# A ring of five expert slots on the chip, hand-ordered engines, half-partition stores and a column-tiled tail in an attention-plus-experts kernel

## The chip, the cores and the metric

The kernel runs on one core of one Trainium2 chip. The metric is the device time of one execution in microseconds (us). The kernel before takes 252.5 us (median; its runs spread from 252.4 to 253.2).

Engine names in the profile: PE is TensorE's matmuls, PEld its weight loads (beside the matmuls: 7.9 us of them in a stage of 16.7 us that PE fills), DVE is VectorE, ACT is ScalarE, POOL is GpSimd. L171 is line 171 of the kernel that the profile belongs to. "MoE" is the expert part of one sequence.

## The reference, cut to what matters

Eight sequences of 576 tokens go through a linear attention with 8 heads of 64 and then, whole, through one of eight experts. The mean of the attention's output picks the expert.

```python
# attention: q, k, v are [8 sequences, 8 heads, 576, 64]
q_s = softmax(q, axis=-1)                 # over the 64 of a head
k_s = softmax(k, axis=2)                  # over the 576 tokens
kv  = einsum('bhsd,bhse->bhde', k_s, v)
x   = einsum('bhsd,bhde->bhse', q_s, kv)  # then [8, 576, 512]
# experts: w1 [8, 512, 1024], w2 [8, 1024, 512]
e_idx  = argmax(x.mean(axis=1) @ w_gate, axis=1)
out[b] = gate_w[b] * (relu(x[b] @ w1[e]) @ w2[e])
```

With the inputs used here the eight sequences draw the experts 2 3 3 1 3 3 4 6, so three of the eight weight loads repeat an expert already drawn.

## The kernel before

Attention runs two sequences ahead of the experts. A sequence is prepared in two halves: exponentials on ScalarE, row sum, reciprocal and multiply on VectorE. TensorE transposes the result, VectorE copies it out as `qt`, and a matmul with `kv` gives `x`. Only TensorE's order is given by hand, one attention step after each MoE step. The compiler orders all other engines.

```python
# attention(b), one half
qs = tensor_reduce(eq, add); qsi = reciprocal(qs)
nc.vector.tensor_tensor(out=eq, in0=eq, in1=qsi..., op=ALU.mult)   # both halves first
...
tps = [bank(t_tag, 2) for g in range(2)]          # two transpose banks
for j in range(J):
    for g in range(2):                            # row groups alternate
        nc.tensor.transpose(out=tps[g]..., in_=eq[r, j], identity=ident[r, r])
...
# routing, then every sequence loads its expert
e_val = nc.values_load(eidx[0:1, 0:1], engines=[ET.Pool], ...)
nc.gpsimd.dma_start(out=w1_sb[...], in_=w1_src[i, h])              # 4 such, then 2 for w2
...
# moe(b): 8 steps of W1, 4 steps of W2 with 128 rows, a tail with 64 rows
nc.scalar.mul(osb[0:rows], po[0:rows], gate[0:rows])
nc.sync.dma_start(out=out[b, st * 128:...], in_=osb[0:rows])       # same queue as the inputs
...
with tc.manual_schedule(engines={ET.PE}):
    for b in range(B):
        ...
        for step, _ in enumerate(moe(b)):
            next(att, None)
```

The softmax here doesn't subtract the row's maximum and nothing guards it: scores larger than these inputs give would overflow.

## Time and profile before

| what | before | from |
|---|---|---|
| median time | 252.5 us | the runs |
| profiled span, mean granted clock | 251.7 us, 0.959 | the cores view |
| first MoE starts | 45.6 us | the timeline |
| lengths of the seven stages after it | 27.3, 43.3, 25.6, 25.6, 24.0, 22.5, 16.7 us | the same |
| last MoE starts | 230.7 us | the same |

A stage runs from the first W1 matmul of one MoE to that of the next. A mixed stage has an attention woven in; the last two stages have none. The second stage holds a hole, which the waits view explains (columns: who waits, for what, us in total, times, longest). One result store had not landed for 19.6 us, so ScalarE could not write the next result, and TensorE stood still behind it for 16.0 us:

```profile
PE hm L243 <- ACT hsb L253: 16.0, 1, 16.0
ACT osb L269 <- DMA out_dram<-osb: 19.6, 1, 19.6
```

The prediction below shows the other lines of this profile.

### The profile page before, as it was taken

What the parts mean: (1) busy time and instruction counts of PE and PEld (TensorE: products, weight loads), DVE (VectorE), ACT (ScalarE), POOL (GpSimd) and SP (SyncE); (2) the same over time, 40 slices, a digit from 0 to 9 for tenths busy, and PEclk for the clock granted to TensorE, in tenths of its full rate; (3) what the DMA queues carried; (4) which work ended last, traced back from release to release, by engine and by line L of the source; (5) the groups of instructions that cost most, each with busy time, mean ns of one, the idle gap of its engine ahead of it and who ended that gap; (6) DMA issues with size and microseconds to landing.
All of it is one profiled execution on the core that took longest, in us unless ns stands there. A gap on an engine that the chain in (4) does not pass through costs nothing.

```text
span 251.7 us, 4145 instructions
## 1 busy us (share of the span) xinstructions
PE 184.3 (73%) x1552; PEld 92.9 (37%) x1552; DVE 131.4 (52%) x365; ACT 91.1 (36%) x130; POOL 52.5 (21%) x73
## 2 busy tenths in 40 slices
PE   0234342887991028799779977997999899999993
PEld 0221221444441004444444444444544454544541
DVE  0699999399411018932993299419723760210300
ACT  3535521335220042535352535353233133344332
POOL 1331451612331000142113211231041006000000
PEclk9999999999997556999999999999999999999999
DMA  6999999999999978669998992299339907993023
GB/s 223 391 392 393 388 296 285 293 283 281 294 282 279 292 204 282 173 174 200 279 316 284 195 240 37 49 177 244 54 74 205 236 11 153 225 188 131 19 83 104
DMA packets 31956, 54.81 MB, mean 218 GB/s; under 512 B 2752, under 2 KB 10944, under 8 KB 31936
## 3 DMA queue, kind: packets, MB, share of 16 engines
q1 hardware_dynamic: 18304, 37.75, 42.5%
q0 software_dynamic: 13056, 16.78, 40.6%
q8 instruction: 12, 0.20, 0.3%
q10 hardware_dynamic: 576, 0.02, 0.1%
q14 instruction: 8, 0.07, 0.1%
HBM read 61.88 MB, written 9.44 MB: 283 GB/s over the span
## 4 chain that ended last, share of the span: by engine, by line
PE 47%; DVE 37%; DMA 11%; ACT 2%; issue 1%; ACTq 1%; DVEq 0%
PE po L264 27%; PE hm L243 12%; DMA out_dram<-osb 8%; DVE qt L154 8%; DVE qs L131 8%; DVE eq L134 7%; DVE xt L184 5%; DVE hsb L255 3%; DMA wg_sb<-in_moe_w_gate_dram 2%; DVE kv L173 2%; PE tk L147 2%; PE x L182 1%; DVE xt L188 1%; PE ht L248 1%; DVE qsi L133 1%
## 5 line engine op out<-in xcount | busy, mean ns | idle before, releaser
L243 PE MATMUL hm<-xt,w_sb 128*128 128x512 f16 x256 | 69.0, 397 | 16.0 <-ACT hsb L253 16.0
L264 PE MATMUL po<-w_sb,hsb 128*128 128x512 f16 (+1 forms) x320 | 73.4, 380 | 0.0
L269 ACT ACTIVATE osb<-po,gate 128x512 f32<-128x512 f32 (+1 forms) x40 | 27.4, 686 | 68.0 <-PE po L264 44.5
L264 PEld LDWEIGHTS <-hsb 128*128 128x128 f16 (+1 forms) x320 | 29.9, 100 | 35.0 <-issue 3.4
L126 POOL CAST va<-v_in 128x1152 f16<-128x1152 f32 x16 | 20.1, 1264 | 94.5 <-PE tk L164 40.6
L154 DVE COPY qt<-tk 128x576 f16<-128x576 f16 x24 | 17.1, 753 | 38.9 <-PE tk L147 38.9
L243 PEld LDWEIGHTS <-w_sb 128*128 128x128 f16 x256 | 20.9, 100 | 39.9 <-issue 21.9
L255 DVE TENSOR_SCALAR hsb<-hm 128x512 f16<-128x512 f32 x32 | 21.9, 686 | 25.7 <-PE hm L243 25.7
L253 ACT ACTIVATE hsb<-hm 128x512 f16<-128x512 f32 x32 | 18.9, 592 | 42.2 <-PE hm L243 42.2
L131 DVE TENSOR_REDUCE qs<-eq 128x18 f32<-128x1152 f16 x16 | 21.5, 1342 | 24.3 <-ACT eq L115 24.3
L211 POOL DMA_DIRECT2D w_sb<-in_moe_w_dram x32 | 19.3, 622 | 64.6 <-DVE gt L225 45.6
L248 PEld LDWEIGHTS <-w_sb 128*128 128x128 f16 x256 | 16.8, 101 | 16.4 <-issue 2.2
L120 ACT ACTIVATE ek<-k_in 128x1152 f16<-128x1152 f32 x16 | 18.5, 1159 | 11.9 <-PE tk L164 8.9
L115 ACT ACTIVATE eq<-q_in 128x1152 f16<-128x1152 f32 x16 | 18.6, 1161 | 11.5 <-DMA q_in<-in_q_dram 5.6
L134 DVE TENSOR_TENSOR eq<-eq,qsi 128x1152 f16<-128x1152 f16 x16 | 21.9, 1368 | 0.1
L164 PE MATMUL tk<-va,ek 64*128 64x129 f16 x288 | 16.0, 246 | 5.0 <-DVE qt L154 2.9
L248 PE MATMUL ht<-xt,w_sb 128*128 128x64 f16 x256 | 18.5, 196 | 0.0
L182 PE MATMUL x<-qt,kv 128*128 128x512 f16 x24 | 9.6, 401 | 10.8 <-DVE pooled L184 5.8
L184 DVE CUSTOM_DVE_ANT_0 xt<-x,ones_f 128x512 f16<-128x512 f32 x24 | 16.4, 685 | 1.6 <-PE tk L183 1.6
L164 PEld LDWEIGHTS <-ek 64*128 64x128 f16 x288 | 11.3, 108 | 7.7 <-issue 6.5
L147 PEld LDWEIGHTS <-eq 64*128 64x128 f16 x288 | 6.5, 103 | 13.4 <-ACT wg_sb L89 9.4
L182 PE MATMUL po<-qt,kv 128*128 128x512 f16 x8 | 4.4, 612 | 9.5 <-DVE kv L173 9.5
(49 smaller groups left out, 107.9 us busy)
## 6 DMA issues: line engine op xcount, KB each, us to landing
q_in<-in_q_dram SPq DMA_DIRECT2D x16, 576.0 KB, 10.6
k_in<-in_k_dram SPq DMA_DIRECT2D x16, 576.0 KB, 11.6
v_in<-in_v_dram SPq DMA_DIRECT2D x16, 576.0 KB, 11.5
w_sb<-in_moe_w_dram POOLq DMA_DIRECT2D x32, 256.0 KB, 7.9
w_sb<-in_moe_w_dram POOLq DMA_DIRECT2D x16, 512.0 KB, 14.6
out_dram<-osb SPq DMA_DIRECT2D x32, 256.0 KB, 4.1
out_dram<-osb SPq DMA_DIRECT2D x8, 128.0 KB, 6.0
wg_sb<-in_moe_w_gate_dram ACTq DMA_DIRECT2D x4, 4.0 KB, 5.4
```

The lines of the kernel that those rows point to most:

```text
L126: nc.gpsimd.tensor_copy(out=va[:, :, 1:].rearrange("p j (n d) -> p n j d", n=2), in_=tiles["v", i].rearrange("p n (j d) -> p n j d", j=J),)
L131: nc.vector.tensor_reduce(out=qs, in_=eq, op=ALU.add, axis=AX.X)
L134: nc.vector.tensor_tensor(out=eq, in0=eq, in1=qsi.unsqueeze(3).to_broadcast([128, J, 2, Dh]), op=ALU.mult,)
L154: nc.vector.tensor_copy(out=qt.rearrange("q (p j) -> q p j", j=J), in_=tps[g].bitcast(FP16)[:, 0:S].rearrange("q (j p) -> q p j", j=J),)
L164: nc.tensor.matmul(kps[g][:, 0:129], lhsT=ek[r, j], rhs=va[r, j], start=(j == 0), stop=(j == J - 1),)
L184: nc.vector.tensor_tensor_reduce(out=xt[:, c, 0:SM], in0=px, in1=ones_f32.to_broadcast([128, SM]), scale=1.0, scalar=0.0, op0=ALU.mult, op ...
L211: nc.gpsimd.dma_start(out=w1_sb[64 * h:64 * h + 64, 2 * i:2 * i + 2, :], in_=w1_src[i, h])
L243: nc.tensor.matmul(phm, lhsT=w1_sb[:, c, fsl], rhs=xt[:, c, 0:SM], start=(c == 0), stop=(c == ND - 1),)
L248: nc.tensor.matmul(pht[:, fc * ST:(fc + 1) * ST], lhsT=w1_sb[:, c, fsl], rhs=xt[:, c, SM:S], start=(fc == 0 and c == 0), stop=(fc == NF - ...
L255: nc.vector.tensor_single_scalar(out=hsb[:, fc, 0:SM], in_=phm, scalar=0.0, op=ALU.max)
L264: nc.tensor.matmul(po[0:rows], lhsT=hsb[:, fc, st * 128:st * 128 + rows], rhs=w2_sb[:, fc, :], start=(fc == 0), stop=(fc == NF - 1),)
L269: nc.scalar.mul(osb[0:rows], po[0:rows], gate[0:rows])
```

## The change

The intent has four parts.

1. Keep the last five experts on the chip in a ring of slots. If the drawn expert is in a slot, skip its load and copy the slot on VectorE into the sequence's own slot.
2. Order all engines by hand, with input loads three half-sequences ahead instead of a sequence and more. Move the ReLUs to ScalarE and most of the multiplies to GpSimd.
3. Store results from 64 partitions at a time, in a token order that makes the `qt` copy dense.
4. Compute the W2 tail of 64 rows as two column halves side by side.

```diff
-    w_pool = ctx.enter_context(tc.tile_pool(name="w", bufs=3))
+    w1_all = consts.tile([128, NS, ND, F], FP16, name="w1_all")    # NS = 5
+    w2_all = consts.tile([128, NS, NF, D], FP16, name="w2_all")
+    BUFS = {"mm": 3, "ht": 1, "kv": 2, "t": 1, "x": 1}             # one transpose bank
...
+        eng = nc.vector if n < 4 else nc.gpsimd
+        eng.tensor_tensor(out=eq, in0=eq, in1=qsi..., op=ALU.mult)
...
-            tps = [bank(t_tag, 2) for g in range(2)]
+            for g in range(2):                                     # one group, then the other
+                tp = bank("mm" if roomy and g == 1 else "t").bitcast(FP16)
...
+            kw = dict(cond=(f_val == 1))                           # load only a fresh expert
+    def fetch(b, w_all):                                           # slot copy on VectorE
+        nc.vector.tensor_copy(out=w_all[:, b % NS], in_=w_all[:, ds(s_val, 1)]...)
...
+            for jj in range(2):
+                nc.sync.dma_start(out=out_p[b, :, 2 * st + jj], in_=osb[64 * jj:64 * jj + 64])
...
+        for fc in range(NF):
+            for dh in range(2):                                    # column-tiled tail
+                nc.tensor.matmul(po[64 * dh:64 * dh + 64, 0:HD], lhsT=hsb[:, fc, SM:S], ...)
...
-    with tc.manual_schedule(engines={ET.PE}):
+    with tc.manual_schedule(engines={ET.PE, ET.DVE, ET.Activation, ET.Pool, ET.SP}):
+        half_now = min(2 * b + (1 if s >= 1 else 0) + (1 if s >= 6 else 0), 2 * B - 1)
+        while prepared[0] <= half_now:                             # ahead of the step's own work
+            prepare_half(prepared[0])
+        if b and s == 6: fetch(b - 1, w1_all)
+        if b and s == 8: fetch(b - 1, w2_all)
+                owed = min(owed + 1.25, NA * (b + 3) - pos[0])     # attention steps per MoE step
```

## The prediction

> **What bounds the kernel now.** I read the page first: busy shares, the 40 slices, the DMA queues, the chain that ended last.
>
> ```profile
> PE 184.3 (73%) x1552; PEld 92.9 (37%) x1552; DVE 131.4 (52%) x365; ACT 91.1 (36%) x130; POOL 52.5 (21%) x73
> PE   0234342887991028799779977997999899999993
> DVE  0699999399411018932993299419723760210300
> DMA  6999999999999978669998992299339907993023
> q1 hardware_dynamic: 18304, 37.75, 42.5%
> q0 software_dynamic: 13056, 16.78, 40.6%
> PE 47%; DVE 37%; DMA 11%; ACT 2%; issue 1%; ACTq 1%; DVEq 0%
> ```
>
> No engine is full; the stages differ. Slices are 6.3 us. To slice 7 (45.7 us) PE works at 0.2 to 0.4 while DVE and DMA are full: a prologue of two attentions. Slices 12 to 14 hold a hole. Slices 15 to 33 mix one expert (MoE) with one attention, DVE alternating with PE. The last two MoEs are pure PE. Then I measured the stages with windows cut at MoE starts.
>
> ```profile
> 20.00:45.70 25.70, 9.31 (x105) 5.55 (x106) 24.31 (x66) 8.77 (x12) 8.68 (x11) 1.00 1.08 335
> 70.50:92.00 21.50, 5.87 (x63) 3.04 (x62) 2.02 (x3) 1.25 (x2) 1.90 (x2) 0.69 1.10 282
> 116.30:141.90 25.60, 22.16 (x195) 11.14 (x196) 16.08 (x45) 11.16 (x16) 6.24 (x8) 1.00 1.04 269
> 214.00:230.70 16.70, 16.70 (x106) 7.91 (x106) 2.77 (x4) 6.42 (x10) 0.00 (x0) 1.00 0.86 190
> ```
>
> Columns: stretch, length, busy PE, PEld, DVE, ACT, POOL, clock, DMA share, GB/s. A pure MoE takes 16.7 us, a mixed stage 25.6 (later 24.0 and 22.5). The hole at 70.5 is one store: the waits view has ScalarE's evacuation 19.6 us behind it, the DMA engines being full with loads ordered long ahead. Last, the timeline of one mixed stage gives the hand-offs.
>
> ```profile
> 117.82 1.16 ACT L115 ACTIVATE eq<-q_in 128x1152 f16<-128x1152 f32 x1
> 119.72 1.34 DVE L131 TENSOR_REDUCE qs<-eq 128x18 f32<-128x1152 f16 x1
> 122.98 0.68 DVE L184 CUSTOM_DVE_ANT_0 xt<-x,ones_f 128x512 f16<-128x512 f32 x1
> 123.72 0.38 PE L182 MATMUL x<-qt,kv 128*128 128x512 f16 x1 [0.73 <-DVE pooled L184]
> ```
>
> Exp 1.16 us and row sum 1.34 us stand in one chain; a second x matmul waits until DVE has emptied the only x bank.
>
> [...]GpSimd's first cast took 1.95 us while DVE's multiply ran from 7.90 to 9.26 us, later ones 1.17.[...]
>
> **The change part by part.**
> *Weights.* Running the reference's routing gives experts 2 3 3 1 3 3 4 6, so 5 of 8 loads remain. The software queue's 40.6% of 251.7 us x 5/8 leaves 64 us of DMA work; with the hardware queue's 107 that is 171 of 252 us instead of 209. Loads run three half-sequences ahead, not a whole sequence and more, so the store hole should vanish: -21 us. Without it this saving lies beside other work.
> *PE work.* [...]Attention stays near 3.6 us a sequence.
> *DVE work.* Leaves: 32 ReLUs (21.9 us) and 12 of 16 multiplies (16.4). Comes: 14 slot copies, run even when nothing is resident[...], and some eight small routing operations a sequence (about 1.2 us each time, 8 x 1.2 = 10). About 11 us less[...].
> *Prologue.* One and a half attentions before the first MoE. DVE's order: half 0 (sum and multiply) to 9.3 us, kv and half 1's preparation to 15.3, qt and xt to 18.5, kv to 20.5, half 2's preparation to 23.4, qt and xt to 26.5, routing to 29, then half 3 with its own preparation to 37. First MoE at about 38 (45.7 before).
> *The hand order in a mixed stage.* I had the compiled order of both kernels listed. PE: W1, kv, W1, transposes, W1, transposes, and so on. DVE: kv evacuation, **row sum of the next half, then the qt copies**. The exp for that sum stands on ScalarE behind the ReLU of the second W1 step, and there is now one transpose bank, so the second transposes wait for the first qt copy. From the end of that W1: ReLU 0.1 + 0.5, exp 1.1, sum 1.4, reciprocal 0.3, [...]hand-off 0.05 = 3.9 us; PE has 0.23 + 0.98 of work meanwhile: **2.7 us of wait**. Half a stage later the same chain has a slot copy in it[...]. Two x matmuls stand back to back on one bank: **0.9**[...]. The gate's matmul waits for routing: 2.95 us from its logits (1.26 in the old trace, plus six operations more and two for the split gate) against one W2 step of 1.75: about **1.4** with hand-offs. Sum 10.2. PE's work: 8 x 0.98 + 4 x 1.73 [...]+ 3.7 = 19.4. A mixed stage comes to 29.6, four more than before.
> *Sum.* 38 prologue; first stage (sixteen attention steps, three preparations, two slot copies) 33.5; second 30; three of 29.6 = 88.8; the last mixed one without its second preparation 25.8; two pure 31.4 to 32; end 3.2: 251. The hole's 21 us and the prologue's 8 would be given back by waits in the stages.
>
> **The rivals.** (A) As worked out, **251 us**: hand order makes row sums stand ahead of what PE needs. For: each duration is in the trace, and the order is in the program. Against: somebody tuned this order, and would have seen such waits; my chain takes every hand-off in full. (B) Half of these waits are hidden, because ScalarE and DVE run ahead or operations overlap: stages of 25 us, **224 us**. (C) PE becomes the bound: stages of 20.5 us, 195, plus some 10 us of late weight landings (in the old trace the second weight matrix landed 12.6 to 22.4 us after issue, and DVE now stands behind it): **205 us**. For: PE work falls and DVE is lighter. Against: one transpose bank and one x bank.[...]
>
> **Range and chances.** Weights 0.55, 0.25, 0.20 for A, B, C give a mean of 0.55 x 251 + 0.25 x 224 + 0.20 x 205 = 235; the middle of the distribution lies higher, as A is the heaviest, so I say 240. The range of 210 to 258 runs from C to A[...]. Faster by over 2% means below 247.5: all of B and C and 0.4 of A, 0.67. Slower (over 257.6): 0.08. Within 2%: 0.25.
>
> **What would show it.** Right: no hole of 20 us; software queue near 10.5 MB; first MoE near 38 us; PE waits of 2 us and more at the transposes, released by the qt copy, twice a stage; the qt copy behind the row sum in the chain of waits; mixed stages near 29 us[...]. Wrong: mixed stages of 20 to 22 us with PE above 90% (C), slot copies above 2 us or waits of DVE for weights (the prediction too low), or a first MoE later than 45 us.

Where the text is cut, it gave figures that no trace of the kernel before shows: what a slot copy, a dense `qt` copy, GpSimd's multiply and the column-tiled tail take, and a fourth rival and a remark that rested on them. So (A) did not have each duration from the trace. The sums still hold the cut terms: waits of 10.2 us (6.6 at the transposes, of which 2.7 at the first with the `qt` copy's term in it; 2.2 at the `x` matmuls; 1.4 at the gate), 19.4 us of PE's work with the tail in it, 29.6 us for a mixed stage, 251 us in all, and some 11 us less work on VectorE. The range's upper end, 258, holds the cut remark. That PE's work falls, in (C), was not shown either.

## The result and the profile after

The changed kernel takes **290.9 us** (median of four runs; the three fast ones from 289.9 to 291.5, a slow one of 298.4) against 252.5. The ratio is 1.150, with a 95% interval of 1.145 to 1.155. All ratios here are the mean time of one kernel's fast runs over that of the other's in the same rounds, so they are not quite the ratio of the medians quoted. The change was predicted faster and is 15% slower.

First the page of the changed kernel: busy time of the engines, three rows of 40 slices (here of 7.2 us), and the software DMA queue.

```profile
PE 197.5 (68%) x1608; PEld 102.6 (36%) x1608; DVE 132.5 (46%) x416; ACT 105.0 (36%) x161; POOL 68.0 (24%) x89
PE   0242376667577296673796649959289688899992
PEclk9999997999599787995997966986759959999999
DMA  7999899499917726997156261410007950798324
...
q0 software_dynamic: 8736, 10.49, 22.7%
```

The load saving came as designed: the software queue moved 10.49 MB instead of 16.78. The DMA row falls to 0 and 1 in the later slices, so transfers are not what bounds the kernel there. PE's row has no hole of several slices any more, but few of its slices are full before the last two MoEs, and two fall to 0.2. The row PEclk has changed: before, the mean granted clock was 0.959, with slices of 0.5 in and just after the hole alone; here it is 0.887, with 0.5 to 0.7 in many stages. The clock has no record before its first change at 42.4 us, and the views count full clock there. The 128x512 matmuls of that time take 0.58 to 0.63 us, as later at half clock (0.38 at full clock), so the mean is too high by this, in both kernels alike.

Next the windows cut at MoE starts (columns: stretch, length, busy PE, PEld, DVE, ACT, POOL, granted clock, DMA share, GB/s): two mixed stages and a pure one.

```profile
148.60:185.10 36.50, 26.82 (x203) 13.24 (x203) 17.07 (x51) 12.87 (x20) 6.76 (x10) 0.81 0.43 130
185.10:222.80 37.70, 28.03 (x204) 13.72 (x203) 17.07 (x51) 12.87 (x20) 9.47 (x10) 0.77 0.18 37
251.80:267.70 15.90, 15.90 (x115) 7.96 (x114) 2.45 (x2) 8.49 (x14) 0.17 (x1) 1.00 0.95 184
```

The six mixed stages, which took 22.5 to 27.3 us before (the hole apart), now take 38.8, 36.6, 33.2, 36.5, 37.6 and 29.1 (the second window above ends 0.1 us late); the pure stage shrank from 16.7 to 15.9. PE counts 26.8 and 28.0 us busy in these two, where a stage before had 22.2, though it has no more to compute: at the clocks of 0.81 and 0.77 its work takes longer. Both things can be seen in the timeline of the first of these stages (columns: start, length, engine, line, what; in brackets the wait before it and who ended it).

```profile
151.71 1.04 PE L293 MATMUL mm<-xt,w_all 128*128 128x512 f16 x4
153.01 1.35 DVE L132 TENSOR_REDUCE qs<-eq 128x18 f32<-128x1152 f16 x1 [1.64 <-ACT eq L126]
155.10 0.64 PE L171 MATMUL t<-ident,eq 64*128 64x64 f16 x9 [2.23 <-DVE qt L175]
155.66 1.89 PE L293 MATMUL mm<-xt,w_all 128*128 128x512 f16 x4
...
166.11 2.94 DVE L280 COPY w_all<-w_all 128x4096 f16 x1 [0.42 <-DVE qsi L134]
169.47 0.63 PE L171 MATMUL t<-ident,eq 64*128 64x64 f16 x9 [5.66 <-DVE qt L175]
173.81 3.60 PE L311 MATMUL mm<-w_all,hsb 128*128 128x512 f16 x8
```

PE waits 2.23 us for a `qt` copy that stands behind a row sum on VectorE, and 5.66 us for one that stands behind a row sum and a slot copy. After each wait the same W1 group takes 1.89 us instead of 1.04, and a W2 step 3.60 instead of the 1.90 that it took before. Windows of 3.41 us, laid so that they meet the clock's own changes, show how the two go together:

```profile
151.63:155.04 3.41, 1.23 (x13) 0.68 (x10) 1.93 (x3) 2.89 (x4) 0.14 (x1) 1.00 0.32 66
155.04:158.46 3.42, 3.15 (x19) 1.58 (x19) 0.69 (x3) 0.60 (x1) 3.08 (x2) 0.50 0.97 347
...
165.28:168.69 3.41, 0.00 (x0) 0.00 (x0) 2.88 (x3) 0.19 (x1) 2.12 (x1) 1.00 0.90 274
168.69:172.11 3.42, 2.64 (x18) 1.42 (x18) 2.41 (x4) 0.15 (x1) 0.00 (x0) 0.50 0.60 222
172.11:175.52 3.41, 2.68 (x10) 0.94 (x8) 1.98 (x8) 0.94 (x2) 0.00 (x0) 0.50 0.02 7
175.52:178.94 3.42, 3.42 (x17) 1.16 (x16) 1.01 (x8) 0.69 (x1) 0.00 (x0) 0.50 0.00 0
178.94:182.35 3.41, 3.15 (x16) 1.35 (x15) 1.20 (x10) 1.08 (x3) 0.22 (x5) 1.00 0.41 94
```

The clock is 1.00 or 0.50 for a whole window and changes only between two; the records of half clock in this trace are 3.413, 6.827 or 10.240 us long, one, two or three windows. PE was idle for 2.18 us of the first window (3.41 less 1.23), and the next one runs at half clock; that one has 0.27 us idle and is followed by full clock. The window that is idle throughout is followed by three at half clock: two of them still have 0.7 to 0.8 us of waits, and only after the third, with none, does the clock return.

I cut the whole changed kernel this way. Every change of its clock before the last MoE's end, 20 in all, lies within 0.05 of a whole number of windows of 3.413 us from the first. 19 windows, 64.9 us, are at half clock. PE was busy for 51.4 us of these, so its work took at most half of that, 26 us, longer for the clock.

Over the whole kernel the waits view names one wait above all, and the groups view shows the slot copies (busy us, mean ns of one, idle before):

```profile
PE t L171 <- DVE qt L175: 45.8, 13, 5.7
```

```profile
L280 DVE COPY w_all<-w_all 128x4096 f16 x14 | 25.0, 1788 | 18.7 <-DMA w_all<-in_moe_w_dram 14.8
```

The copies' mean of 1788 ns mixes two sizes: 1.23 us alone (the shortest is 1226 ns) and 2.94 us when one starts just after GpSimd's multiply (one that started 0.98 us after it took 2.22), as here in the timeline of an earlier stage:

```profile
96.08 2.12 POOL L136 TENSOR_TENSOR eq<-eq,qsi 128x1152 f16<-128x1152 f16 x1 [4.64 <-ACT hsb L304]
96.34 2.94 DVE L280 COPY w_all<-w_all 128x4096 f16 x1 [0.43 <-DVE qsi L134]
```

The copy ends 1.08 us after the multiply, which is roughly its time alone.

### The profile page after: what moved, and what is told of

The parts are those of the page before. It is cut to its first block, busy times and chain, and to the rows that moved or that the text cites. A ratio compares the mean times of both kernels' runs of the same rounds, so it can differ in the third digit from the quotient of the medians.

```text
span 288.6 us, 4585 instructions
## 1 busy us (share of the span) xinstructions
PE 197.5 (68%) x1608; PEld 102.6 (36%) x1608; DVE 132.5 (46%) x416; ACT 105.0 (36%) x161; POOL 68.0 (24%) x89
## 3 DMA queue, kind: packets, MB, share of 16 engines
q0 software_dynamic: 8736, 10.49, 22.7%
## 4 chain that ended last, share of the span: by engine, by line
PE 42%; DVE 12%; ACT 4%; issue 2%; DVEq 0%; ACTq 0%
PE mm L311 17%; PE mm L293 15%; DVE w_all L280 3%; DVE qs L132 3%; ACT eq L126 3%; PE mm L324 2%; DVE xt L184 2%; PE x L182 2%; PE kv L152 2%; PE t L171 2%; PE ht L298 2%; DVE qt L175 1%; DVE qsi L134 1%; ACT hsb L302 1%; PE x L196 0%
## 5 line engine op out<-in xcount | busy, mean ns | idle before, releaser
L293 PE MATMUL mm<-xt,w_all 128*128 128x512 f16 x256 | 75.0, 424 | 0.0
L302 ACT ACTIVATE hsb<-mm 128x512 f16<-128x512 f32 x64 | 38.1, 595 | 85.2 <-PE mm L293 85.2
L311 PE MATMUL mm<-w_all,hsb 128*128 128x512 f16 x256 | 66.9, 416 | 0.0
L171 PE MATMUL t<-ident,eq 64*128 64x64 f16 x270 | 15.2, 207 | 45.8 <-DVE qt L175 45.8
L316 ACT ACTIVATE osb<-mm,gate 128x512 f32<-128x512 f32 x32 | 22.0, 686 | 54.8 <-PE mm L311 33.8
L136 POOL TENSOR_TENSOR eq<-eq,qsi 128x1152 f16<-128x1152 f16 x12 | 25.4, 2115 | 68.7 <-DVE qsi L134 64.1
L311 PEld LDWEIGHTS <-hsb 128*128 128x128 f16 x256 | 25.1, 105 | 36.9 <-issue 14.4
L280 DVE COPY w_all<-w_all 128x4096 f16 x14 | 25.0, 1788 | 18.7 <-DMA w_all<-in_moe_w_dram 14.8
L293 PEld LDWEIGHTS <-w_all 128*128 128x128 f16 x256 | 21.8, 105 | 27.8 <-issue 12.9
L298 PEld LDWEIGHTS <-w_all 128*128 128x128 f16 x256 | 17.8, 105 | 18.3 <-issue 5.7
L159 DVE RECIPROCAL icv<-kv 128x1 f32<-128x1 f32 x32 | 5.2, 163 | 38.8 <-PE kv L152 38.8
L298 PE MATMUL ht<-xt,w_all 128*128 128x64 f16 x256 | 19.3, 201 | 0.0
```

The lines of the kernel that those rows point to most:

```text
L136: eng.tensor_tensor(out=eq, in0=eq, in1=qsi.unsqueeze(3).to_broadcast([128, J, 2, Dh]), op=ALU.mult,)
L171: nc.tensor.transpose(out=tp[:, 64 * j:64 * j + 64], in_=eq[r, j], identity=ident[r, r],)
L280: nc.vector.tensor_copy(out=w_all[:, b % NS], in_=w_all[:, ds(s_val, 1)].rearrange("p o c f -> p (o c) f"))
L293: nc.tensor.matmul(phm, lhsT=w1_sb[:, c, fsl], rhs=xt[:, c, 0:SM], start=(c == 0), stop=(c == ND - 1),)
L298: nc.tensor.matmul(pht[:, fc * ST:(fc + 1) * ST], lhsT=w1_sb[:, c, fsl], rhs=xt[:, c, SM:S], start=(fc == 0 and c == 0), stop=(fc == NF - ...
L302: nc.scalar.activation(out=hsb[:, fc, 0:SM], in_=phm, func=AF.Relu)
```

## The experiments

**Theory 1**: the hand order of the vector work makes PE wait at the second transposes (row sum and slot copy ahead of the `qt` copy), and these waits cost twice, because the clock halves after them. **Rival 2**: the waits belong to TensorE's own order and its single transpose bank, whatever the vector order. **Rival 3**: the ring itself is the loss. Twelve kernels ran, all with correct results; the ratio is always to the kernel before.

### Row sums after the qt copies

```diff
     def prepare_half(n): ...            # exponentials stay where they were
+    def sums_half(n): ...               # row sum, reciprocal, multiply
...
         next(att[b])
+        sum_now = min(2 * b + (1 if s >= 2 else 0) + (1 if s >= 7 else 0), 2 * B - 1)
+        while summed[0] <= sum_now:
+            sums_half(summed[0])
```

> Only VectorE's order is changed: the row sum, reciprocal and multiply of the next half stand behind the two qt copies instead of ahead of them; exps, slot copies and everything else stay. Theory of the hand order (the sum ahead of the qt copy makes TensorE wait at the second transposes, 2.2 us in the first half of a stage and 5.7 in the second): the 45.8 us of waits at the transposes fall below 10; about 1 us comes back per stage at the x matmuls in the first half, and in the second half the second slot copy now runs beside GpSimd's multiply, so some 4 to 5 us turn up at the x matmul there. Total about 268 us. Rival (the slot copies alone make the waits): first half as before, total 285 to 290.

Measured: **264.8 us**, ratio 1.048 (1.043 to 1.054), clock 0.951. From the waits view:

```profile
PE x L185 <- DVE pooled L187: 34.3, 14, 5.9
PE t L174 <- DVE qt L178: 4.4, 6, 1.7
```

The waits for `qt` fell from 45.8 to 4.4 us and the kernel gained 26 us by an edit of order alone. A new wait took 34.3 us: the second `x` matmul now stands behind the slot copy, 4.82 us in each steady stage. The steady mixed stages went from 33 to 38 us to 30.7.

### Slot copies later, row sums where they were

```diff
+        if b and s == 6:
+            fetch(b - 1, w1_all)        # ahead of the next half's row sum
         half_now = ...
-        if b and s == 6: fetch(b - 1, w1_all)
-        if b and s == 8: fetch(b - 1, w2_all)
         next(att[b])
+        if b and s == 9: fetch(b - 1, w2_all)
```

> Only the slot copies move: W1's goes ahead of the row sum, into the time in which VectorE waits for the exp, W2's behind the x evacuations. Theory of the slot copies: none runs beside GpSimd's multiply, so all take 1.23 us (now 2.95 in four to six of them); the second wait at the transposes falls from 5.7 to the 2.2 of the first, and with it most of the time at half clock behind it: mixed stages from 36 to about 30 us, total about 250 us. Rival (the row sum alone makes the wait, copies are hidden anyway): the second wait stays above 4 us, total above 275.

Measured: 272.4 and 271.6 us in two fast runs, 277.3 and 277.4 in two slow ones. All copies took 1.23 us, as they no longer met the multiply, and the wait of 5.66 us became 2.04 to 2.24. Yet the total missed the expectation by some 22 us. In two stages a wait of the same 2.24 us ended at 147.5 and at 192.5 us, and what came after differs (the first two lines are the 1.5 us after each wait; the other two are windows of the 3.413 us grid):

```profile
147.50:149.00 1.50, 1.45 (x12) 0.81 (x12) 0.46 (x1) 0.00 (x0) 1.50 (x1) 0.50 0.92 273
192.50:194.00 1.50, 1.50 (x18) 0.88 (x18) 0.46 (x1) 0.11 (x1) 1.50 (x1) 1.00 0.00 0
```

```profile
143.65:147.06 3.41, 1.66 (x22) 1.05 (x21) 1.67 (x3) 3.19 (x4) 0.00 (x0) 1.00 0.27 47
191.43:194.85 3.42, 1.75 (x19) 1.01 (x19) 1.96 (x6) 1.42 (x3) 2.12 (x1) 1.00 0.00 0
```

After the first wait PE did 12 matmuls at 0.50, after the second 18 at 1.00. The first left 1.75 us idle in its window; the second was cut by a boundary at 191.43, and its two windows had 1.20 and 1.66 us idle. In the traces of this kernel and of the changed one together (135 windows from the first MoE on), every window with more than 1.66 us idle at full clock was followed by half clock, none with less than 1.62 was, and the clock returned only after windows with at most 0.31 us idle. So here a wait of 2.24 us trips the clock or not by where it falls, and short waits afterwards keep it down: windows with 0.49 and 0.74 us idle did. Seven of the fourteen kernels, cut in the same way (some 430 windows), agree: between 1.63 and 1.73 us idle both outcomes occur, and the clock came back after at most 0.31 us idle and stayed down from 0.49 on.

### Both edits

> Both edits together. If the two orders are the cause, waits at the transposes are under 1 us each, no wait is long enough to drop the clock (granted clock above 0.97 over the span), mixed stages take 24 to 26 us and the total is 225 to 235 us, faster than both kernels. If something else bounds the stages (DMA, the gate's chain, GpSimd), the total stays above 245.

The edit is the two above together. Measured: **245.0 us**, ratio 0.968 (0.965 to 0.972), five of six runs fast; the profile is of a slow run (246.2 us, clock 0.969). The kernel is now faster than before by 3%. No wait in a steady stage is above 1.5 us, and the clock holds:

```profile
131.40:157.60 26.20, 21.43 (x203) 11.49 (x201) 14.93 (x51) 12.64 (x20) 6.76 (x10) 1.00 0.60 181
```

The expectation of 225 to 235 was missed by 10, and 245 is the edge that the rival named. The three steady stages took 26.2, 26.2 and 25.6 us, close to the 24 to 26 expected; the three ahead of them took 32.3, 31.4 and 28.8, with four windows at half clock and waits of up to 3.3 us for the gate. At full clock, PE's work in a mixed stage is 21.4 us, where the prediction had 19.4.

### Idle matmuls into the waits of the changed kernel

This leaves the order as it is and fills part of the waits with matmuls of no use (8 ahead of the short wait, 20 ahead of the long one), so that the clock has no idle time to fall in.

```diff
+                if b and g == 1:
+                    dm = bank("x")
+                    for _ in range(8 if i == 0 else 20):
+                        nc.tensor.matmul(dm, lhsT=blkmask, rhs=warm, start=True, stop=True)
                 tp = bank("mm" if roomy and g == 1 else "t").bitcast(FP16)
```

> The changed kernel with its order as it is, but TensorE runs 8 idle 128x512 matmuls into the free x bank ahead of the first waiting transposes of a stage and 20 ahead of the second (1.7 and 4.3 us at full clock), so that it waits the same but is not idle. Results stay right. Theory of the clock (after a wait of some 2 us and more TensorE works at half clock for 3 to 9 us, some 31 us in all over the mixed stages): granted clock above 0.96, the first W2 step in 1.7 instead of 3.4 us, mixed stages from 36 to about 31, total about 260 us. Rival (the chain of VectorE sets the time, the clock only follows): total within 3 us of 290.

Measured: **280.8 us**, ratio 1.104 (1.096 to 1.113), clock 0.975. A kernel with 196 matmuls more is 10 us faster. The stage that took 36.5 us:

```profile
148.00:180.30 32.30, 27.57 (x231) 14.02 (x229) 16.98 (x51) 12.75 (x20) 6.76 (x10) 1.00 0.49 147
```

The two stages with the lowest clocks went from 36.5 and 37.6 to 32.3 us each, the second from 36.6 to 35.2, the one that had kept its clock at 0.90 from 33.2 only to 32.5, and the first and the sixth became 1.0 and 1.7 longer with the useless matmuls. So the clock's part is shown, but its size is below the 31 us that the expectation implied: its total of about 260 was missed by 21. PE's busy time falls from 197.5 us in the changed kernel to 181.1 with both order edits, on the same 1608 matmuls; that kernel still has four windows at half clock. So the slow clock made PE's work in the changed kernel at least 16 us longer, and by the bound above at most 26. Not all of this is lost time: the slower W2 steps cover the wait for the gate, 0.3 us in the stage above and 0.9 here at full clock. The two clearest stages lost 4.2 and 5.3 us to the clock.

### The order of the other engines left to the compiler

```diff
-    with tc.manual_schedule(engines={ET.PE, ET.DVE, ET.Activation, ET.Pool, ET.SP}):
+    with tc.manual_schedule(engines={ET.PE}):
```

> The changed kernel with one part undone: only TensorE's order is given by hand, as in the kernel before; the order of VectorE, ScalarE, GpSimd and the queue is left to the compiler's scheduler. TensorE's own list is the same, instruction for instruction. Theory 1 (the hand order of the vector work, row sums ahead of the qt copies, is what makes the waits): the waits for qt fall from 45.8 us to under 25 and the time to 255 to 275, with a clock above 0.92. Rival (the waits come from TensorE's own order and the single transpose bank, so anybody's vector order makes them): 283 to 295, with the qt waits within a fifth of 45.8.

Measured: **276.7 us**, ratio 1.092 (1.088 to 1.096), clock 0.885. From the waits view:

```profile
PE t L171 <- DVE qt L175: 22.9, 7, 14.3
```

and, in the longest of these waits, from VectorE's timeline, just ahead of the `qt` copy at 78.79:

```profile
77.65 1.23 DVE L280 COPY w_all<-w_all 128x4096 f16 x1 [8.55 <-DMA w_all<-in_moe_w_dram]
```

TensorE's order is unchanged and the wait halved, which speaks against rival 2; the time missed the expected range by 2 us and the clock was not better. The compiler has its own fault: one wait of 14.3 us in the first stage, where it put slot copies, which wait for a weight load to land, ahead of `qt` copies. Hand order is not the fault as such: this hand order costs 14 us more than the compiler's, and the reordered one costs 32 us less (245.0 against 276.7).

### Is the ring worth its copies?

All eight loads, no slot copies, the changed kernel's order kept:

```diff
-            kw = dict(cond=(f_val == 1))
+            kw = {}
...
     def fetch(b, w_all):
-        sidx = seqs[b][2]
-        if sidx is None:
-            return
+        return
```

> The changed kernel with its order, but without the reuse of slots: every sequence loads its expert (8 loads instead of 5, 12.6 MB more read) and no slot copy runs; the slot search stays. Theory (the saved loads lie off the path, the copies on it): as e2 or a little better, second wait at the transposes about 2.2 instead of 5.7, total 268 to 276 us. Rival (the saved loads are worth time): late weights or inputs show as waits for DMA and the total is 285 or more.

Measured: 262.2 and 263.7 us in two fast runs (267.2 and 273.3 in slow ones, among them the profiled one), ratio 1.040 (1.035 to 1.045). That is better than expected. The software queue moves 16.78 MB instead of 10.49, so in this order the ring saves 6.3 MB of loads (the 12.6 of the expectation is twice too much) and loses 27 us.

### The kernel before, with its stores on another queue

The prediction credited the change with 21 us for a hole that hangs on one store. This asks what the hole is worth by itself.

```diff
-            nc.sync.dma_start(out=out[b, st * 128:st * 128 + rows, :], in_=osb[0:rows])
+            nc.scalar.dma_start(out=out[b, st * 128:st * 128 + rows, :], in_=osb[0:rows])
```

> The kernel before with one edit: the result's stores are issued from ScalarE's queue, not behind the input loads in SyncE's. Theory (the hole of 21 us at 70.5 is one store standing behind loads ordered long ahead in the same queue): the wait of 19.6 us behind that store falls below 5, total 230 to 238 us. Rival (the DMA engines are full there, so whatever is late, a store, an input or a weight, stops the kernel): the hole moves to another wait for DMA and the total stays above 244.

Measured: **244.0 us**, ratio 0.966 (0.962 to 0.971). One word gains 3.4%, but only half of the hole:

```profile
PE hm L243 <- ACT hsb L253: 5.3, 1, 5.3
```

The wait of 16.0 us became 5.3, and the stage 32.7 us instead of 43.3. The expected range was missed by 6 us, and the total lies just above the 244 that the rival named. An input load for `v` now has 11% of the chain that ended last; in the prediction's sum the whole hole was gone.

### Building on the better order

Four runs follow from the one with both edits. The first gives one attention step to each MoE step instead of 1.25 and puts the gate's exponential ahead of the slot search.

```diff
-                owed = min(owed + 1.25, NA * (b + 3) - pos[0])
+                owed = min(owed + 1.0, NA * (b + 3) - pos[0])
```

> On top of e3_both: one attention step per MoE step instead of 1.25, so no two x matmuls stand back to back on the one bank, and the exp, reciprocal and split of the gate stand on VectorE ahead of nothing but the slot search, which now comes after the max for the exp. Theory (what is left of waits in e3's stage, 1.40 twice and 1.47 at the gate out of 26.2 us, is set by order): x waits under 0.5 each, gate under 0.4, mixed stages 22.5 to 23.5 us, total 222 to 230 us. Rival (VectorE or GpSimd is now full and the waits turn up elsewhere): stages stay above 25, total above 240.

Measured: **236.2 us**, ratio 0.933 (0.930 to 0.937). It missed the range by 6 us, and its clock is down to 0.945. The gate's matmul still waits 2.2 to 3.0 us in most mixed stages, because its neighbours are now W1 steps of 1 us, shorter than the W2 steps that had covered it.

The second transposes both row groups in alternation, as the kernel before did, with the second group in the `x` bank.

```diff
-            for g in range(2):
-                tp = bank("mm" if roomy and g == 1 else "t").bitcast(FP16)
-                for j in range(J):
+            tps = [bank("t").bitcast(FP16), bank("mm" if roomy else "x").bitcast(FP16)]
+            for j in range(J):
+                for g in range(2):
```

> On top of e5: the nine transposes of both row groups alternate again as in the kernel before, the second group in the x bank, which is free at that time. In the kernel before eighteen took 0.41 to 0.44 us, in the changed one nine take 0.42. If the pairing is what made them short, TensorE's work falls by 0.8 us a stage and the wait of 0.44 at the second transposes goes: stages about 21.5 to 22, total 5 to 8 us below e5. If the length is a matter of how the trace models ends, nothing changes.

Measured: **228.7 us**, ratio 0.905 (0.900 to 0.909), 7.5 us better, as expected. Nine transposes of one row group take 0.43 us in the timeline of the changed kernel, and 18 alternating ones take 0.44 here, as in the kernel before where nothing held them up: the second nine cost next to nothing when they alternate. The stages took 23.4 to 27.0 us, more than the 21.5 to 22 expected.

The third takes the ring out of this version, by the same edit as above.

> e6_pairs (228.71 us) with all eight experts loaded and no slot copy; the search stays. Theory 1, the saved loads are off the path in the good order too, and the copies cost only what TensorE was seen to wait for them (1.7 us once, plus some of the row sums that stand behind them): 224 to 229 us, software queue 16.8 MB instead of 10.5. Theory 2, with the mixed stages shortened to 24 us the loads begin to matter (inputs and weights share the engines): 232 us or more, with TensorE waiting for v or for a weight. Theory 3, the copies still cost much, as in e7: 215 to 222.

Measured: **219.7 us**, ratio 0.866 (0.862 to 0.870): theory 3 of the expectation. TensorE was seen to wait only 1.7 us for a slot copy by name, but the gate's wait shrank with it, from 2.23 to 1.04 us in a steady stage, since the second copy of 1.23 us stood ahead of the routing on VectorE. With the shorter wait the clock stayed at 1.00 in three steady stages, where the version with the ring had 0.93 in three of its last four mixed stages. The loads do show elsewhere: TensorE waited once for 6.1 us behind a result store.

The fourth moves the gate's matmul one step later, and the fifth does both.

```diff
+        yield
         pb = bank("x")
         nc.tensor.matmul(pb[:, 0:2], lhsT=ones_row, rhs=hl, start=True, stop=True)
...
-    NA = 12
+    NA = 13
...
-        for _ in range(NA + 6):
+        for _ in range(NA + 7):
```

> e6_pairs with the gate's broadcast matmul one matmul step later (13 attention steps a sequence instead of 12, one more ahead of the first MoE). Theory 1, the gate wait (18.4 us in eight waits, 2.2 each and once 5.0) is on the path and one step of 0.98 us takes about 1 us off each: six mixed waits x 1.0, less 1 us for the longer start, 222 to 225 us, with gate waits of about 1.2. Theory 2, the wait only moves to the next product that VectorE owes (vector work fills the time): 227 to 230, with the gate wait gone and another grown.

Measured: **224.8 us**, ratio 0.886 (0.883 to 0.890); theory 1's range held. The waits view shows what was given back:

```profile
PE x L270 <- DVE hl L264: 12.7, 7, 4.2
PE mm L299 <- DVE w_all L286: 9.0, 7, 1.7
```

The gate's wait fell from 18.4 to 12.7 us, and the first W1 step now waits for its slot copy in seven stages, 9.0 us.

> e9 and e10 together: if the two are independent, 228.7 less both gains. Theory 1: 219 to 225. If both fight over the same VectorE time: the better of the two.

Measured: **207.4 us**, ratio 0.816 (0.812 to 0.820), below the expected range and 8 us below the sum of the two gains (228.7 - 9.0 - 3.9 = 215.8). Without slot copies the shorter gate wait is not given back. From its page and windows:

```profile
PE   0053332699999999999999959999999999999990
```

```profile
80.10:100.40 20.30, 19.97 (x205) 10.73 (x203) 12.70 (x49) 12.61 (x21) 10.47 (x10) 1.00 1.12 291
```

From the first MoE on PE is full but for one dip, where a result store held ScalarE for 4.9 us. A mixed stage takes 20.3 us with 20.0 of PE work at full clock. This version, with all eight loads, beats the kernel before by 18% and the changed one by more. The DMA share is now 1.12 in that stage and stores come back in the chain that ended last, so here fewer loads could begin to matter; that was not tried.

## Why the prediction was wrong

**What held.** The first rival had the cause of the waits right: it named the place (the second transposes), the releaser (the `qt` copy behind the row sum) and the slot copy in the second one. It had 10.2 us of waits a mixed stage; the three middle stages of the changed kernel have 10.3, 9.7 and 9.7. That the sum is so close is partly luck, as the waits view of the stage from 148.5 us shows:

```profile
PE x L182 <- DVE pooled L184: 1.5, 2, 0.7
PE x L264 <- DVE hl L260: 0.3, 1, 0.3
```

The sum had 2.2 for the `x` matmuls and 1.4 for the gate; the two waits for `qt`, 2.23 and 5.66 us, were 6.6 in it. The errors cancel. The first MoE began at 39.9 us (predicted 38) and the software queue moved 10.49 MB (10.5). A slot copy alone took 1.23 us, a `qt` copy 0.39 to 0.46 us (about 0.75 before), GpSimd's multiply 2.1 us (1.37 on VectorE before), and the column-tiled tail, from its first matmul to the next group's, 1.00 us (1.85 before). The hole was gone. VectorE's work did not fall, though: it was busy for 132.5 us (131.4 before), where some 11 us less were forecast; the slot copies alone took 25.0, where 14 of 1.23 us would be 17.

**What failed.** The profiled span is 288.6 us, 37.6 more than that rival's sum of 251. The three middle stages took 107.4 us instead of 88.8; with the waits as forecast, the excess lies in TensorE's busy time, 22.9, 26.8 and 28.0 us instead of 19.4 each.

1. *"Sum 10.2. PE's work: 8 x 0.98 + 4 x 1.73 ... + 3.7 = 19.4."* This adds waits to work at full speed. The waits also slow the work: the clock halves after many of them (19 windows at 0.50), which the sum has no term for. In the three middle stages this is 13.5 us of busy time (77.7 less three times the 21.4 of the next point), in the whole kernel 16 to 26, and the run with idle matmuls shows the cause by itself. The trace of the kernel before had it: around the wait of 16.0 us its clock stood at 0.50 for 20.48 us, the four W1 matmuls after the wait took 1.86 us instead of 1.04, and the prediction's own table has 0.69 for that stretch. Having derived waits of 2.7 us and more, the prediction should have asked what they do to the clock, even though that one long wait does not show what a short one does.
2. *The 19.4 itself.* At full clock it is 21.4 (the window of the version with both edits), 2 us a stage and some 12 in six. The MoE's part was right (a pure stage has 15.9 us), so the term that was too small is the attention, 3.7 instead of 5.5. The prediction's second table had it: the old mixed stage's busy PE, 22.2 us, less a pure MoE's 16.7, is 5.5.
3. *"Half a stage later the same chain has a slot copy in it."* The sum had too little for this wait. It was 5.66 us in the steady stages, since the copy met GpSimd's multiply and took 2.94 us instead of 1.23. The prediction had this contention outside its sum, as an estimate that rested on no trace. In the middle stages smaller waits elsewhere made up for it.
4. The start and the end cost 2 us more each than the sum had, the two early stages 5.3 and 6.6 more, the last mixed one 3.3. How these three stages divide into clock, work and waits was not taken apart.

**The choice that turned the sign.** The working's own figure was 251 us, but 0.45 of the weight went to rivals at 224 and 205, on the ground that somebody had tuned the order and that hand-offs might overlap. The prediction shows no line of a trace for that, while its waits, but for the cut terms, were worked out from such lines. Even so, 251 alone would have missed the result: the sign came from the weights, the size from the missing clock term.

**The rivals in the light of the runs.** The second theory of the experiments, TensorE's own order, falls as the cause of the `qt` waits: the vector order alone removes 41 of 46 us of them. It is not without cost: two of the later edits, one attention step to a MoE step (made together with a change of the gate's order) and the alternating transposes in a second bank, change TensorE's own list, and they gained 9 and 7.5 us. The ring is a loss of its own, 27 us in the changed order (part of that through waits and clock) and 9 to 17 us in the better ones (228.7 against 219.7, 224.8 against 207.4). The prediction's third rival, stages of 20.5 us bound by PE, was possible with most of these parts: it is what the last version reaches, at 20.3 us, with another order and no ring.

**What stays open.** No run set the phase of a wait against the clock's windows on purpose. Runs of one kernel can differ widely here: the one without slot copies had 262.2 to 273.3 us at clocks of 0.946 to 0.887. Whether that is the phase of the windows was not tested, so figures from two fast runs are rough. The half-partition stores, the ReLUs on ScalarE and the multiplies on GpSimd were not tried by themselves, and the last version was not tried with fewer loads.

## What to carry to other kernels

When every engine is ordered by hand, write down for each wait of the busiest engine what stands ahead of its releaser on the releaser's engine; moving a row sum behind a copy was worth 26 us here, and two order edits turned a 15% loss into a 3% gain. Look in the trace whether a wait costs twice, by itself and by the clock after it: here every window of 3.413 us with more than 1.73 us idle at full clock was followed by half clock, which lasted until a window with at most 0.31 us idle (the seven kernels that were cut into windows). Ask what waits for the bytes that are saved: in the orders tried here little did, and the copies that bought them stood in the line of VectorE's work that TensorE waited for, at a cost of 9 to 27 us.
